# Recurrence with fewer load buffers, the scaling one step further ahead, one group of products moved, and half as many warm products of twice the length

## The chip, the cores and the metric

The program runs on one core of one Trainium2 chip. The metric is the device time of one execution in microseconds, as the median of several runs. Times inside an execution are taken from one profiled execution and counted from the start of its span.

## The reference

Three stages follow each other. The first is a linear-attention recurrence over 768 positions, for 4 sequences, 8 heads and a head size of 48:

```python
for t in range(S):
    cur = np.einsum('bhd,bhe->bhde', u[None] * kt, vt)
    y[:, :, t] = np.einsum('bhd,bhde->bhe', rt, state + cur)
    state = w[None, :, :, None] * state + np.einsum('bhd,bhe->bhde', kt, vt)
```

Its output, 3072 tokens of 384 numbers, goes through a mixture of 8 experts (hidden size 1024). Each token with a positive skip score goes to the expert with the highest logit, and `gate * (relu(x @ w1[e]) @ w2[e])` is added to it. The third stage is a soft mixture of 8 experts with 4 slots each: softmaxes of `x @ phi` over tokens and over slots, two products per slot, and a combination over slots. Everything is float32.

## The kernel before

All engines' programs are written out by hand: inside `manual_schedule` each engine executes its instructions in the order in which the Python code issues them. The part that matters here is the loop `for i in range(NT)` with 24 steps. Step `i` handles one block of 128 positions (`c`) of one sequence (`b`), all 8 heads together. For one block the work is:

- `load(j)` (L509 to L519) issues two transfers on SyncE's queue: `rk`, the block of r and k, into one of `NRK = 5` buffers `rkb`, and `kv` into one of 5 buffers with the tag `kvt`. A transfer into a buffer is issued when the last reader of its former contents is done, and SyncE's queue is in order, so it holds up all transfers behind it. In step `i` the loads of block `i + 3` are issued; the last reader of a `kvt` buffer is the second half of `av` for its block (TensorE, L753), one step after the block's own.
- `prep(j)` (L630) scales r and k by decay powers into the tile `rks` (VectorE, L635 and L636) and multiplies r with k into `pd` (GpSimd, L638). `prepk(j)` makes `kt` from `kv` (GpSimd, L644). Both are called in step `j - 1`.
- `scores(j)` (L646): 16 products `sc` (L656), which the chip's records show as 32 pairs of a weight load and a product, then for the block before `inter` (L734) and the first half of `av` (L753), then the argument `between`, then the products `ud` (L666) and their copy `dts` (ScalarE, L668).
- `trx` (transposes, L764), `upd` (products into `ud`, L679), `bonus` (a transpose, L682), `moved` (copy by ScalarE, L695), the second half of `av`.
- `past(j)` (VectorE, L705) takes the masked scores out of `sc` into `at`, and `amask(j)` (VectorE, L714) puts the diagonal in. `sc` has one buffer in PSUM, so the products `sc` of step `i + 1` wait for `past(i)`; `av` of step `i + 1` waits for `amask(i)`.

Every fourth step has routing work besides: `route1` (8 records of products `lgt`, L837, copied by ScalarE to `lgs`, L838), `route2` (transposes of `lgs`), and in the three steps after it many short VectorE instructions (`route2b`, `gates`, `places`, `route4`, `hots`). `route1(4)` is the `between` of step 21 and `route1(5)` that of step 23.

Ahead of the loop `warm(n, w)` (L498) issues `n` products of a constant with `4 * w` columns that nobody reads: `warm(44, 48)` first, and `warm(5, 48)` in step 0. From step 20 on, `wload` issues the expert weights on SyncE's queue behind the last loads of the recurrence, and `stored` writes finished tokens (`x_d`) on the same queue. Behind the loop the router finishes, tokens are gathered for the experts, and from 139.5 us on TensorE runs the experts' products.

Of the kernel before, what the change touches and what calls it, by code (L numbers as in the profile page):

```python
# [8 lines left out]
F32 = mybir.dt.float32  # L9
# [10 lines left out]
P = 128  # L20
NC_ = S // P
NT = B * NC_
DM = H * D
# [7 lines left out]
PR = 112  # L31
HT = P // 2
NWR = 7
NWARM = 44
NVX = 10
WLO, WHI = 0.8, 1.1
HF = F // 2
# [437 lines left out]
def tile_main(ctx, tc, rk, kv, wu, wcat, phi, w1, w2, v1, v2, r_in, k_in, v_in, w_in, u_in, wcn, out, dbg=None, force=False):  # L475
    nc = tc.nc
# [13 lines left out]
    PE_, DVE_, ACT_, POOL_, SP_ = (mybir.EngineType.PE, mybir.EngineType.DVE, mybir.EngineType.Activation, mybir.EngineType.Pool, mybir.EngineType.SP)  # L490
    mst = ExitStack()
    mst.enter_context(tc.manual_schedule(engines={PE_, DVE_, ACT_, POOL_, SP_}))
    NRK = 5
    ones = fp.tile([P, P], BF16, name="ones")
    nc.vector.memset(ones, float(E))

    def warm(n, w=P):

        wp = ps.tile([P, 2, 4 * P], F32, tag="y", name="wp")[:, 0, 0 : 4 * w]
        for _ in range(n):  # L500
            nc.tensor.matmul(wp, ones, ones[:, 0:w].rearrange("p (o n) -> p o n", o=1).to_broadcast([P, 4, w]), start=True, stop=True)  # L501

    warm(NWARM, 48)
    rkb = [kp.tile([PR, 2, 4, P], F32, name=f"rkb{i}") for i in range(NRK)]
    wt = kp.tile([PR, 2, 4], F32, name="wt")
    nc.sync.dma_start(out=wt, in_=wu)
# [1 line left out]
    T = {}  # L508

    def load(j, first=True, last=True):  # L510
        c, b = divmod(j, B)
        if first:
            t = T[j] = {"rk": rkb[j % NRK]}
            nc.sync.dma_start(out=t["rk"], in_=rk[c, b])
        if not last:
            return
        t = T[j]
        t["kv"] = wk.tile([P, 2, DM], F32, tag="kvt", bufs=5, name=f"kvt{j}")
        nc.sync.dma_start(out=t["kv"], in_=kv[c, b])  # L519

    load(0, last=False)
# [105 lines left out]

    yts = {}

    def prep(j):  # L630
        t = T[j]
        rkt = t["rk"]
        rks = wk.tile([PR, 2, 4, P], F32, tag="rks", bufs=3, name=f"rks{j}")
        t["rs"], t["ks"] = rks[:, 0], rks[:, 1]
        nc.vector.tensor_mul(rks[:, 0], rkt[:, 0], prt)  # L635
        nc.vector.tensor_mul(rks[:, 1], rkt[:, 1], pkt)  # L636
        t["pd"] = wk.tile([PR, 4, P], F32, tag="pd", name=f"pd{j}")
        nc.gpsimd.tensor_mul(t["pd"], rkt[:, 0], rkt[:, 1])  # L638

    def prepk(j):  # L640
        t = T[j]
        if j < NT - B:
            t["kt"] = wk.tile([P, DM], F32, tag="kt", name=f"kt{j}")
            nc.gpsimd.tensor_mul(t["kt"], t["kv"][:, 0], pktok.rearrange("t h d -> t (h d)"))  # L644
# [183 lines left out]
    def route1(g, pool=ps, tag="r"):  # L828
        c, (j0, nb) = g, GR[g]
        r = RT[c] = {}  # L830
        lgt = pool.tile([P, nb * P], F32, tag=tag, name=f"lgt{c}")
        r["lgs"] = ry.tile([P, nb * P], F32, tag="lgs", bufs=2, name=f"lgs{c}")
        yt, b0 = yts[j0 // B], j0 % B
        for q in range(2):
            for s2 in range(2):
                p = 2 * s2 + q
                nc.tensor.matmul(lgt[64 * s2 : 64 * s2 + 64, :], wcs[:, p, :], yt[:, p, b0 : b0 + nb, :].rearrange("d b t -> d (b t)"), start=(q == 0), stop=(q == 1))  # L837
        nc.scalar.copy(r["lgs"], lgt)  # L838
# [183 lines left out]
    pa = Banks(u=[(ps, "t", 1)])  # L1022
    if True:
        for i in range(NT):
            if i + 3 < NT:
                load(i + 3)
            rc, rb = divmod(i - 5, B)
            rok = 0 <= rc < NC_ - 1
            if i == 0:
                decays()  # L1030
                warm(5, 48)
                prep(0)
                prepk(0)
                for hf in range(2):
                    r0 = 64 * hf
                    nc.vector.tensor_copy(usel[r0 : r0 + D, :, hf : hf + 1], wt[r0 : r0 + D, 1, :].rearrange("p (a o) -> p a o", o=1))
            scores(i, lambda: route1(i // 2 - 6) if i in (21, 23) else None)
            if i > 1:
                trx(i - 2)
            if rok and rb == 3 or i == 22:  # L1040
                route3(rc, place=T[i]["rp"])
            if rok and rb == 2 and rc < 4:
                route2(rc)
            if i == 21:
                route2(4)
            if i == 23:
                route2(5)
            if rok and rb == 1 and rc < 4:
                route1(rc)
            if i == 0:  # L1050
                prep(1)
                prepk(1)
                for ts in spf:
                    for t in ts:
                        nc.gpsimd.memset(t[:, 4 * D :], 0.0)
            elif i + 1 < NT:
                prep(i + 1)
                prepk(i + 1)
            if i > 0:
                state(i - 1)  # L1060
            upd(i)
            if i == 22:
                c4pt = ps.tile([P, P], F32, tag="r", name="c4pt")
                nc.tensor.transpose(c4pt, c4t.rearrange("p q s -> p (q s)"), ident)
            bonus(i)
            moved(i)
            if i > 0:
                av(i - 1, 1)
            if i in (13, 17, 21, 22):
                gathered(len(LI))  # L1070
            past(i)
            if i == 22:
                nc.vector.tensor_reduce(mcs[:, 0:1], c4pt, axis=AX.X, op=ALU.max)
                dgt = rt.tile([32, 32], F32, tag="dg", bufs=1, name="dgt")
                nc.vector.tensor_scalar(dgt, ident[0:32, 0:32], mcs[0:32, 0:1], None, op0=ALU.mult)
                amask(22)
                weave("pgpgg", g=gates(4), p=places(4))
                tokens(4, nc.gpsimd)
                hots(4, range(4), nc.gpsimd)
            decayed(i)  # L1080
            if i == 21:
                nc.vector.tensor_reduce(cmax, cmg.rearrange("t g s -> t s g"), axis=AX.X, op=ALU.max)
                c4t = fourfold(nc, "t", rt, cmax)
                amask(21)
                route2b(4)
            elif rb == 0 and 1 <= rc < 4:
                route4(rc - 1)
            if i % B and 9 <= i < 22:
                hots(i // B - 2, (i % B,) if i < 20 else (2, 3), nc.vector if i < 20 else nc.gpsimd)
            if i not in (21, 22):  # L1090
                amask(i)
            if rok and rb == 2 and rc < 4:
                route2b(rc)
            if rok and rb == 3:
                weave("gpgpg", g=gates(rc), p=places(rc))
                count(rc)
                tokens(rc, nc.gpsimd)
                hots(rc, (0,) if rc < 3 else (0, 1), nc.vector if rc < 3 else nc.gpsimd)
                if rc == 3:
                    route4(3)  # L1100
            if i == 8:
                wok = rt.tile([PR, 2, 4], F32, tag="wok", bufs=1, name="wok")
                nc.vector.tensor_scalar(wok[:, 0], wt[:, 0, :], WLO, None, op0=ALU.is_ge)
                nc.vector.tensor_scalar(wok[:, 1], wt[:, 0, :], WHI, None, op0=ALU.is_le)
                wmn = mk.tile([PR, 1], BF16, name="wmn")
                nc.vector.tensor_reduce(wmn, wok, axis=AX.XY, op=ALU.min)
            if 20 <= i < 23:
                wload(i - 20)
            if i % B == 1 and 9 <= i < 25:
                stored(i - 9, B)  # L1110
            if i == 22:
                stored(16, B)
            if 3 <= i < 7:
                constants(i)
            if i == 4:
                odd = rt.tile([P, NT], F32, tag="odd", bufs=1, name="odd")
                nc.vector.tensor_reduce(odd[:, 0:1], ident.rearrange("p (a r) -> p r a", r=2)[:, 1:2], axis=AX.X, op=ALU.add)
                nc.vector.tensor_scalar(odd[:, 1:2], odd[:, 0:1], float(-NT), None, op0=ALU.mult)
                tf = rt.tile([P, 2, NT], F32, tag="tf", bufs=1, name="tf")
                nc.scalar.copy(tf, tj_i)  # L1120
                nc.vector.tensor_scalar(tj[:, 0], tf[:, 0], float(NT), odd[:, 1:2], op0=ALU.mult, op1=ALU.add)
                nc.vector.tensor_sub(tj[:, 1], tf[:, 1], tj[:, 0])
                nc.gpsimd.iota(ipl.bitcast(I32), pattern=[[E, CAP]], base=-NOROW, channel_multiplier=0)
                nc.gpsimd.tensor_copy(ipl, ipl.bitcast(I32))
                for t in tok:
                    nc.gpsimd.memset(t, 0.0)
            if i == 6:
                sf = rt.tile([P, E], F32, tag="sf", bufs=1, name="sf")
                nc.vector.tensor_reduce(sf, ident.rearrange("p (q r s) -> p s q r", q=4, s=E)[:, :, :, 0:2], axis=AX.XY, op=ALU.add)
                nc.scalar.copy(selb, sf)  # L1130
# [543 lines left out]
```

## Time and profile before

| | us |
|---|---|
| median of 3 runs | 350.14 |
| lowest and highest | 348.92, 354.14 |
| the profiled execution | 348.07 |
| its span, first to last instruction | 346.3 |

The profile gives for each engine when its instructions ran and what ended the idle time before them. `PE` is TensorE's products, `PEld` its weight loads, `DVE` VectorE, `ACT` ScalarE, `POOL` GpSimd, `SP` SyncE; a `q` behind a name is an engine's queue. A wait put down to "issue" is one for which the profile shows no releaser. The granted clock is 1.00 at 2.4 GHz and 0.50 at 1.2 GHz. The execution's own time is 1.77 us longer than its span.

### The profile page before, as it was taken

The numbers are of one execution on the slowest core, as the hardware profiler recorded it, in microseconds if no ns is written. First come the engines' busy times: TensorE is split into PE (matmuls) and PEld (weight loads), VectorE is DVE, ScalarE is ACT, GpSimd is POOL, SyncE is SP. The second block draws the span as 40 slices with busy tenths as digits, with TensorE's granted clock in tenths as the row PEclk, the third lists the DMA queues.
The fourth block names the chain that finished last, engine by engine and source line by source line (L and its number), as shares of the span: only waits on it lengthen the run. The fifth ranks groups of instructions, "written<-read, shape, count | busy, mean of one in ns | idle before, by whom it ended". The sixth has DMA issues, their size and how long they took to land.

```text
span 346.3 us, 10440 instructions
## 1 busy us (share of the span) xinstructions
PE 321.4 (93%) x4326; PEld 263.9 (76%) x4326; DVE 226.1 (65%) x510; ACT 159.5 (46%) x353; POOL 139.8 (40%) x181
## 2 busy tenths in 40 slices
PE   8699998999998999999999999999999999999950
PEld 8477776767775782999999999998999998534540
DVE  6637676896969865776675848575676845226850
ACT  3235454444543463554645546464645543121360
POOL 3939685776844544804324232525224002200000
PEclk9969999999999998999999999999999999899995
DMA  7976667684879944899788787878866749779096
GB/s 233 287 220 190 187 189 255 199 269 141 279 191 310 387 163 158 266 310 315 252 288 303 239 281 255 263 257 296 294 197 215 254 124 377 256 268 324 10 338 210
DMA packets 45735, 85.29 MB, mean 246 GB/s; under 512 B 3838, under 2 KB 26672, under 8 KB 45680
## 3 DMA queue, kind: packets, MB, share of 16 engines
q1 hardware_dynamic: 43024, 80.63, 70.8%
q0 software_dynamic: 2128, 3.74, 3.9%
q8 instruction: 36, 0.59, 0.7%
q10 hardware_dynamic: 528, 0.16, 0.2%
q14 instruction: 19, 0.16, 0.1%
HBM read 74.49 MB, written 10.10 MB: 244 GB/s over the span
## 4 chain that ended last, share of the span: by engine, by line
PE 79%; DVE 12%; issue 3%; ACT 2%; POOL 1%; ACTq 0%; DVEq 0%
PE yp L1291 7%; PE yp L1292 6%; PE yp L1293 6%; PE hp L1266 6%; PE hp L1269 6%; PE hp L1267 6%; PE yp L753 4%; PE ehp L216 4%; PE sc L656 3%; PE lgt L837 3%; PE ud L679 3%; PE trp L764 3%; PE yp L734 2%; PE wp L501 2%; PE ud L666 2%
## 5 line engine op out<-in xcount | busy, mean ns | idle before, releaser
L1266 PE MATMUL hp<-xhl,wa 128*128 128x240 f32 x192 | 46.1, 282 | 0.2 <-issue 0.2
L1291 PE MATMUL yp<-wb,hh 128*128 128x384 f32 x128 | 45.2, 353 | 0.0
L1004 DVE TENSOR_TENSOR wa<-w,wa 128x768 fp32r<-128x768 f32 x32 | 30.5, 955 | 22.4 <-ACT wa L1016 22.3
L1267 PE MATMUL hp<-xhl,wa 128*128 128x240 f32 x192 | 44.6, 275 | 0.0
L1292 PE MATMUL yp<-wb,hh 128*128 128x384 f32 x128 | 43.0, 336 | 0.0
L1293 PE MATMUL yp<-wb,hl 128*128 128x384 f32 x128 | 42.9, 335 | 0.0
L1197 POOL DMA_INDIRECT xg<-x_d,idg x16 | 19.9, 1242 | 51.9 <-DVE x L1299 38.1
L638 POOL TENSOR_TENSOR pd<-rkb 112x512 f32<-112x512 f32 x24 | 31.1, 1295 | 18.6 <-PE ud L666 15.3
L1321 POOL DMA_INDIRECT lt_d<-lsr,ids x16 | 17.7, 1106 | 50.2 <-ACT xhl L1256 28.3
L1266 PEld LDWEIGHTS hp<-xhl,wa 128*128 128x128 f32 x192 | 36.2, 189 | 0.5 <-ACT dsbv L135 0.5
L1267 PEld LDWEIGHTS hp<-xhl,wa 128*128 128x128 f32 x192 | 36.2, 189 | 0.0
L714 DVE COPY_PREDICATED at<-ih,ud 128x512 f32<-128x512 int32 x24 | 17.7, 738 | 26.0 <-ACT us L695 16.5
L1004 DVE TENSOR_TENSOR wb<-w,wb 128x768 fp32r<-128x768 f32 x32 | 30.5, 953 | 2.1 <-ACT wb L1016 1.7
L1016 ACT CAST wb<-w 128x768 fp32r<-128x768 f32 x32 | 26.8, 838 | 9.5 <-PE yp L1293 5.5
L753 PE MATMUL yp<-at,kvt 64*48 64x64 f32 (+3 forms) x800 | 27.7, 250 | 1.0 <-DVE at L714 0.4
L1276 ACT ACTIVATE hh<-hp 128x480 fp32r<-128x480 f32 x32 | 18.3, 572 | 22.2 <-PE hp L1269 20.0
L1277 DVE SCALAR_TENSOR_TENSOR hl<-hp,hh 128x480 fp32r<-128x480 f32 x32 | 20.9, 654 | 9.7 <-ACT hh L1276 9.2
L1016 ACT CAST wa<-w 128x768 fp32r<-128x768 f32 x32 | 26.9, 840 | 0.0
L1291 PEld LDWEIGHTS yp<-wb,hh 128*128 128x128 f32 x128 | 24.0, 188 | 3.6 <-issue 3.5
L1269 PE MATMUL hp<-xhl,wa 128*128 128x240 f32 x192 | 26.7, 275 | 0.0
L656 PE MATMUL sc<-rks 48*64 48x128 f32 (+1 forms) x768 | 22.1, 252 | 4.5 <-DVE at L705 2.3
L753 PEld LDWEIGHTS yp<-at,kvt 64*48 64x48 f32 (+1 forms) x800 | 22.2, 125 | 5.3 <-issue 1.6
(346 smaller groups left out, 697.1 us busy)
## 6 DMA issues: line engine op xcount, KB each, us to landing
w<-in_w_dram SPq DMA_DIRECT2D x32, 768.0 KB
v<-in_v_dram SPq DMA_DIRECT2D x29, 768.0 KB
rkb<-in_rk_dram SPq DMA_DIRECT2D x24, 448.0 KB
kvt<-in_kv_dram SPq DMA_DIRECT2D x24, 384.0 KB
x_d<-x SPq DMA_DIRECT2D x5, 768.0 KB
out_dram<-ob SPq DMA_DIRECT2D x5, 768.0 KB
x<-in_v_dram SPq DMA_DIRECT2D x2, 768.0 KB
x_d<-x SPq DMA_DIRECT2D x2, 384.0 KB
```

Source lines behind the costliest of these rows:

```text
L638: nc.gpsimd.tensor_mul(t["pd"], rkt[:, 0], rkt[:, 1])
L656: nc.tensor.matmul(sc[c0 : c0 + HT, g, blocks(p, z), :], ks[r0 : r0 + D, p, HT * z : HT * z + HT], rs[r0 : r0 + D, p, HT * z :], start=Tru ...
L753: nc.tensor.matmul(d, kvt[s0 : s0 + HT, 1, h * D : h * D + m], w, start=(c == ph == z == 0), stop=(ph == z == 1))
L1004: nc.vector.tensor_sub(lv, sl, hv.bitcast(F32))
L1016: nc.scalar.copy(hv, sl)
L1266: nc.tensor.matmul(hp[:, f, 0:ROOM], hi[:, k, fs], xh[:, k, 0:ROOM], start=(k == 0 and f == 0), stop=False)
L1267: nc.tensor.matmul(hp[:, f, 0:ROOM], lo[:, k, fs], xh[:, k, 0:ROOM], start=False, stop=False)
L1269: nc.tensor.matmul(hp[:, f, 0:ROOM], hi[:, k, fs], xl[:, k, 0:ROOM], start=False, stop=(k == 2 and f == 1))
L1277: nc.vector.scalar_tensor_tensor(l, p, 0.0, h.bitcast(F32), op0=ALU.max, op1=ALU.subtract)
L1291: nc.tensor.matmul(YP[e][bl], hh[:, f, bs], hi[:, f, :], start=st, stop=False)
L1292: nc.tensor.matmul(YP[e][bl], hh[:, f, bs], lo[:, f, :], start=False, stop=False)
L1293: nc.tensor.matmul(YP[e][bl], hlo[:, f, bs], hi[:, f, :], start=False, stop=en)
```

## The change

The `rkb` buffers go from 5 to 3 and the `kvt` buffers from 5 to 4. The scaling leaves `prep` for a function `scaled`, with 4 buffers for `rks` in place of 3. `scaled(i + 2)` is called in step `i`: behind `past(i)` from step 3 on, behind `amask(i)` in steps 0 to 2 (there `scaled(0)` and `scaled(1)` stand where `prep` had them). `load(3)` moves behind the first `prep` and `prepk`, since it now reuses the first `rkb` buffer. `route1(4)` moves from the middle of `scores(21)` to behind it. `warm(44, 48)` becomes `warm(22, 96)` and `warm(5, 48)` becomes `warm(2)` with 512 columns.

```diff
-NWARM = 44
+NWARM = 22
...
-    NRK = 5
+    NRK = 3
...
-    warm(NWARM, 48)
+    warm(NWARM, 96)
...
-        t["kv"] = wk.tile([P, 2, DM], F32, tag="kvt", bufs=5, name=f"kvt{j}")
+        t["kv"] = wk.tile([P, 2, DM], F32, tag="kvt", bufs=4, name=f"kvt{j}")
...
+    def scaled(j):
+        if j >= NT:
+            return
+        t = T[j]
+        rkt = t["rk"]
+        rks = wk.tile([PR, 2, 4, P], F32, tag="rks", bufs=4, name=f"rks{j}")
+        t["rs"], t["ks"] = rks[:, 0], rks[:, 1]
+        nc.vector.tensor_mul(rks[:, 0], rkt[:, 0], prt)
+        nc.vector.tensor_mul(rks[:, 1], rkt[:, 1], pkt)
+
     def prep(j):
         t = T[j]
         rkt = t["rk"]
-        rks = wk.tile([PR, 2, 4, P], F32, tag="rks", bufs=3, name=f"rks{j}")
-        t["rs"], t["ks"] = rks[:, 0], rks[:, 1]
-        nc.vector.tensor_mul(rks[:, 0], rkt[:, 0], prt)
-        nc.vector.tensor_mul(rks[:, 1], rkt[:, 1], pkt)
...
-            if i + 3 < NT:
+            if 0 < i < NT - 3:
                 load(i + 3)
...
-                warm(5, 48)
+                warm(2)
+                scaled(0)
                 prep(0)
                 prepk(0)
+                load(3)
...
-            scores(i, lambda: route1(i // 2 - 6) if i in (21, 23) else None)
+            scores(i, lambda: route1(5) if i == 23 else None)
+            if i == 21:
+                route1(4)
...
+                scaled(1)
                 prep(1)
...
             past(i)
+            if i > 2:
+                scaled(i + 2)
...
+            if i <= 2:
+                scaled(i + 2)
```

VectorE's order in steps 7 and 8, before; the number behind a tile's name is its block, and L635 and L636 are the scaling:

```order
L635 TENSOR_TENSOR rks8_880<-rkb3_132,prt_212 112x512
L636 TENSOR_TENSOR rks8_880<-rkb3_132,prt_212 112x512
L705 TENSOR_TENSOR at7_841<-sc7_824,mh_192 128x2x256
L714 COPY_PREDICATED at7_841<-ih_193,ud7_860 128x2x256
...
L901 SCALAR_TENSOR_TENSOR oh0_923<-lgp0_873,m20_921 128x32
L635 TENSOR_TENSOR rks9_983<-rkb4_133,prt_212 112x512
L636 TENSOR_TENSOR rks9_983<-rkb4_133,prt_212 112x512
L705 TENSOR_TENSOR at8_945<-sc8_928,mh_192 128x2x256
L714 COPY_PREDICATED at8_945<-ih_193,ud8_964 128x2x256
```

The same place after the change, where the scaling is L637 and L638, `past` L711 and `amask` L720:

```order
L711 TENSOR_TENSOR at7_817<-sc7_800,mh_168 128x2x256
L637 TENSOR_TENSOR rks9_882<-rkb0_107,prt_188 112x512
L638 TENSOR_TENSOR rks9_882<-rkb0_107,prt_188 112x512
L720 COPY_PREDICATED at7_817<-ih_169,ud7_836 128x2x256
...
L907 SCALAR_TENSOR_TENSOR oh0_899<-lgp0_849,m20_897 128x32
L711 TENSOR_TENSOR at8_921<-sc8_904,mh_168 128x2x256
L637 TENSOR_TENSOR rks10_985<-rkb1_108,prt_188 112x512
L638 TENSOR_TENSOR rks10_985<-rkb1_108,prt_188 112x512
L720 COPY_PREDICATED at8_921<-ih_169,ud8_940 128x2x256
```

The two scaling instructions of a step stand behind `past` in place of ahead of it, and are for the block after the next; `amask` stands behind both as before.

TensorE's order in the middle of step 21, before; `lgt4` are the products of `route1(4)`, `ud21` those whose copy `dts21` is transposed in the last row:

```order
L753 MATMUL yp20_2222<-at20_2128,kvt20_1817 48x64 x4
L837 MATMUL lgt4_2239<-yt4_1895,wcs_140 64x512 x4
L666 MATMUL ud21_2246<-pd21_2169,usel_142 32x128 x4
L764 MATMUL trp19_2253<-ident_149,yt4_1895 128x112 x4
L865 MATMUL lgp4_2259<-ident_149,lgs4_2240 128x128 x4
L682 MATMUL ud21_2246<-ident_149,dts21_2251 128x128
```

The same place after the change:

```order
L759 MATMUL yp20_2198<-at20_2104,kvt20_1793 48x64 x4
L672 MATMUL ud21_2215<-pd21_2142,usel_118 32x128 x4
L843 MATMUL lgt4_2222<-yt4_1868,wcs_116 64x512 x4
L770 MATMUL trp19_2229<-ident_125,yt4_1868 128x112 x4
L871 MATMUL lgp4_2235<-ident_125,lgs4_2223 128x128 x4
L688 MATMUL ud21_2215<-ident_125,dts21_2220 128x128
```

`ud21` and `lgt4` change places; what stands between `lgt4` and the transposes `lgp4` that need its copy is now `trp19` alone.

## Rows read from the trace of the kernel before

**Rows 1.** Time windows of the whole program: busy us by engine (instructions), TensorE clock, DMA share, GB/s
```profile
28.00:124.00 96.00, 90.69 (x2229) 68.42 (x2229) 74.86 (x194) 45.72 (x121) 63.89 (x85) 1.00 0.76 241
...
139.50:300.00 160.50, 160.38 (x1204) 152.30 (x1208) 105.60 (x195) 84.96 (x166) 50.78 (x54) 1.00 0.81 271
```

**Rows 2.** Timeline of the start: start, length, engine, line; wait in brackets
```profile
9.49 1.28 POOL L638 TENSOR_TENSOR pd<-rkb 112x512 f32<-112x512 f32 x1
...
9.84 0.64 PE L679 MATMUL ud<-kvt,kt 128*64 128x48 f32 x16 [0.43 <-POOL kt L644]
...
14.57 0.51 PE L656 MATMUL sc<-rks 48*64 48x128 f32 x12
...
17.30 1.01 PE L656 MATMUL sc<-rks 48*64 48x64 f32 x19 [2.22 <-issue]
...
24.38 0.54 PE L753 MATMUL yp<-at,kvt 64*64 64x128 f32 x10 [0.32 <-issue]
...
29.77 0.42 PEld L679 LDWEIGHTS ud<-kvt,kt 128*64 128x64 f32 x12 [0.25 <-issue]
```

**Rows 3.** The page's list of DMA queues: packets, MB, share of 16 engines
```profile
q8 instruction: 36, 0.59, 0.7%
```

**Rows 4.** The page's list of transfers: KB of one
```profile
rkb<-in_rk_dram SPq DMA_DIRECT2D x24, 448.0 KB
kvt<-in_kv_dram SPq DMA_DIRECT2D x24, 384.0 KB
```

**Rows 5.** Timeline of SyncE's queue at the start
```profile
8.29 0.33 SPq L514 DMA_DIRECT2D rkb<-in_rk_dram  x1
...
15.29 0.77 SPq L514 DMA_DIRECT2D rkb<-in_rk_dram  x1
...
23.38 0.37 SPq L514 DMA_DIRECT2D rkb<-in_rk_dram  x1
```

**Rows 6.** Time windows from the start, and around the half clock
```profile
0.00:10.70 10.70, 9.14 (x114) 8.25 (x114) 7.26 (x24) 3.27 (x10) 5.50 (x17) 1.00 0.83 237
0.00:17.30 17.30, 12.97 (x221) 11.12 (x222) 11.66 (x31) 5.13 (x15) 11.37 (x30) 0.98 0.91 260
0.00:24.40 24.40, 19.75 (x350) 16.56 (x350) 14.35 (x36) 7.53 (x21) 13.64 (x32) 0.86 0.87 240
17.30:23.40 6.10, 6.10 (x109) 5.01 (x112) 1.70 (x3) 1.92 (x5) 2.27 (x2) 0.50 0.79 208
23.40:27.00 3.60, 3.28 (x92) 2.45 (x87) 1.59 (x3) 1.52 (x5) 1.55 (x2) 1.00 0.76 232
```

**Rows 7.** TensorE's waits from 28 to 124 us: total us, times, longest
```profile
PE sc L656 <- DVE at L705: 2.3, 5, 0.9
PE yp L734 <- issue: 0.7, 1, 0.7
PE ud L679 <- issue: 0.7, 1, 0.7
PE yp L753 <- DVE at L714: 0.4, 1, 0.4
```

**Rows 8.** A window inside the recurrence, of steps 7 to 9
```profile
45.00:55.20 10.20, 9.14 (x264) 7.30 (x256) 9.71 (x32) 5.12 (x13) 8.58 (x13) 1.00 0.78 239
```

**Rows 9.** Instructions that write or read the scaled tile: ns min/median/max
```profile
L635 DVE TENSOR_TENSOR rks<-rkb,prt x24: 667/677/687, 6.7 to 116.6; 112x512 f32<-112x512 f32 x24
```

**Rows 10.** Timeline of steps 21 to 23
```profile
108.02 0.90 PE L656 MATMUL sc<-rks 48*64 48x128 f32 x32 [0.88 <-DVE at L705]
...
110.01 1.94 PE L837 MATMUL lgt<-yt,wcs 112*64 112x512 f32 x8 [0.32 <-DVE ltt L957]
...
118.51 0.90 PE L656 MATMUL sc<-rks 48*64 48x128 f32 x32 [0.58 <-DVE at L705]
```

**Rows 11.** Timeline of the warm products
```profile
1.13 6.29 PE L501 MATMUL wp<-ones 128*128 128x192 bf16 x44 [1.13 <-DVE ones L495]
```

**Rows 12.** A window after the last loads of the recurrence
```profile
125.00:129.00 4.00, 3.74 (x84) 3.52 (x76) 3.12 (x15) 2.46 (x8) 1.30 (x2) 1.00 0.02 7
```

## The prediction

> **What bounds the kernel now.** I read the time windows first. From 139.5 us to 300 TensorE is busy for 160.38 of 160.50 us [rows 1]; nothing of the change stands there, so that part keeps its length and what is won earlier passes through. From 28 to 124 us, inside the recurrence, TensorE is busy for 90.69 of 96 us [rows 1], so about 5 us are open there at most. The start is the other place. In the timeline the reader sees TensorE stop after 12 of the 32 products of `sc` of step 2 and go on at 17.30 us after 2.22 us of "issue", which means that no engine and no data is named as the cause [rows 2]. Then its clock: 0.50 from 17.3 to 23.4 us, 1.00 behind it [rows 6]. A product with its weight load takes 6.10 / 109 = 0.056 us in the slow stretch and 3.60 / 92 = 0.039 us behind it.
>
> What is it waiting for? The next "issue" waits of this kind stand at 24.38 and 29.77 us [rows 2]. By the product counts of the windows, 350 - 221 = 129 products start between the resumption at 17.30 and shortly after that at 24.38 [rows 6], so a block is 128 products, or 256 instructions with their weight loads. The queue named "instruction" moves 0.59 MB in 36 packets, 16 KB each [rows 3]; if one packet is one block, an instruction has 64 bytes. I read the stops as program code that comes late, behind the data transfers.
>
> The transfers fit that. I take it that a block is asked for when the one before it begins, 128 products earlier. For the stop that ends at 17.30 this is about 9.84 us [rows 2]. By then SyncE has issued 6 `rk` and 5 `kv` [rows 5], which are 4608 KB or 4.72 MB [rows 4], and 237 GB/s x 9.84 us = 2.33 MB have moved [rows 6]: 2.4 MB stand ahead, and the block takes 7.5 us. For the next, asked for at 17.30, 7 and 6 are issued, 5.57 MB, 4.50 MB are moved, 1.07 MB stand ahead and it takes 7.1 us until 24.38. For the third, at 24.38, 8 and 7, 6.42 MB, 5.86 moved, 0.56 ahead, and 5.4 us until 29.77. With less ahead it comes sooner.
>
> The Trainium skill says otherwise in "Runtime: NRT & Kernel Launch", section "Instruction fetch mechanics": instructions come in 16 KiB blocks of 256, the next is fetched while the present one runs, and the crossing is mostly hidden. The block size agrees with the counts here; that it is hidden does not agree with 2.22 us at 17.30. By its rule the term of the start below would be zero.
>
> **The change part by part.**
>
> *Warm products.* 44 x 192 columns become 22 x 384 and 5 x 192 become 2 x 512: 8448 columns as before, and 1024 for 960. The first group takes 6.29 us [rows 11], and I leave its length as it is. What goes is 25 products, so each block border falls 25 products later in the work.
>
> *Fewer load buffers.* The fourth `rk` now reuses the first buffer; the sixth did so before and was issued at 8.29 us [rows 5], so the fourth `rk` and `kv` are issued at 8.3 to 9 us. The fifth `rk` waits for the second `pd`, which ends at 9.49 + 1.28 = 10.77 us [rows 2]. The block in question is asked for 25 products later than before, 9.84 + 25 x 0.039 = 10.8 us. By then 4 and 4 are issued, 3.41 MB, and 237 x 10.7 = 2.54 MB are moved [rows 4, 6]: 0.87 MB ahead, or 1.33 if the fifth `rk` gets in first. Between the two measured blocks (0.56 MB 5.4 us, 1.07 MB 7.1 us) that is 6.4 us, so it arrives at about 17.2; with 1.33 MB at 17.9. TensorE gets to this border 25 products after 15.08 us (17.30 - 2.22), at 16.1: a stop of 1.1 us, between 0 and 1.8, in place of 2.22. Before, the same place in the work was reached at 17.30 + 25 x 0.056 = 18.7. The gain is 18.7 - 17.2 = 1.5 us.
>
> *Clock.* The slow stretch followed TensorE's stop. Of it 23.4 - 18.7 = 4.7 us are left behind that place, 84 products, and at full clock they would take 84 x 0.017 = 1.4 us less. A stop of 1.1 us may or may not cost the clock; I take half, 0.7 us, with ends 0 and 1.4. The stops of 0.32 and 0.25 us [rows 2] become shorter with less ahead of them: 0.3. Start together: 1.5 + 0.7 + 0.3 = 2.5 us, from 0.5 (late block, clock lost) to 4.6 (no stop at all).
>
> *Scaling a step ahead.* The two instructions take 0.68 us each [rows 9] and run as often as before. They go from ahead of `past` to behind it, so `past` ends up to 1.3 us earlier and `sc` of the next step need not wait. That wait is 2.3 us over five steps [rows 7]. Two of them are 0.88 us in step 21 and 0.58 in step 23 [rows 10]. In step 21 the products `lgt` wait for VectorE anyway (0.32 us on L957), and VectorE has no less to do ahead of L957, so 0.3 comes out. In step 23 no scaling is left to do and all 0.6 comes out. The other three, 0.8 us, lie in stretches such as 45.0 to 55.2, where VectorE is busy for 9.71 of 10.20 us [rows 8]. There it has the same instructions to run up to the last `amask`, for which `av` waits, and TensorE waited 0.4 us for one already [rows 7]. The wait moves from `past` to `amask`, and I count 0. If VectorE had slack, all 0.8 would come out; if the scaling holds `amask` back, the same is lost.
>
> *Step 21.* `lgt` of `route1(4)` behind `ud`: the same products, and TensorE can run `ud` while `lgt` waits. This is the 0.3 counted above, not another. The copy of `lgt` now has only `trx` to hide behind ahead of the transposes; the price is between 0 and 0.4 us, and I take 0.
>
> *Block borders later on.* From 28 to 124 us there are 2229 / 128 = 17 borders. Two of them cost 0.7 us each [rows 7]. All of them move by 25 products, and so against the transfers that each step issues. Some of 1.4 us goes, and other borders get late. Above all the expert weights, issued behind the last `kv`, go out a step later: the `kv` buffers are 4, not 5. So the borders of the last three steps meet them. Price from -1.4 to +2.0; I take 0. The weights themselves have room: the transfers are idle at 0.02 from 125 to 129 us [rows 12], nearly the step of 96 / 20 = 4.8 us by which they are later.
>
> **Sum.** 2.5 + 0.9 = 3.4 us off the profiled execution's 348.07 us (span 346.3, 1.77 around it): 344.7. The three runs shown are 348.92, 350.14 and 354.14; the profiled execution is 0.9 below the lowest and 2.1 below the median. I add 1.5 of this and forecast 346.2 us, 1.1% below the median of 350.14. About 2% is what a measurement of this kernel can tell from no change: under 343.1 us is faster, over 357.1 slower.
>
> **The rivals.**
>
> *The stop goes altogether and the clock holds.* For it: the queue is emptier by 4.72 - 3.41 = 1.3 MB less what moves in 1 us. Against it: 0.87 MB ahead is near the 1.07 MB of a block that took 7.1 us. Then the start gives 4.6, and with 0.9 and half of the 1.4 us of later borders 6.2: 341.9 in the profiled execution, 343 as a median.
>
> *Nothing comes out.* The block waits behind the fifth `rk`, the clock is lost again, `amask` takes over the waits of `past`, and new borders cost what old ones did. 0.5 + 0.9 - 1.4 = 0: 349.5 us.
>
> *The stop at 17.30 is not late code.* Then 25 fewer products and an emptier queue change nothing at the start, and 0.9 is left: 347.2 in the profiled execution, 348.7 as a median. Against it: the spacing of exactly one packet's worth of instructions. This is what the page's rule in the Trainium skill comes to.
>
> *Loads too late: slower.* The `rk` of block j + 5 is issued behind the `kv` that waits for `av` at the end of step j + 1, and the scaling needs it in the middle of step j + 3, where before there were more than two steps more. That is 1.5 steps, 7 us at 4.8 us a step. A step's two transfers are 832 KB, 3.5 us at 241 GB/s [rows 4, 1]; a store of `x_d` ahead of them (as large) makes it 7 us, with the landing still to come. The scaling then holds up `amask` on VectorE. If that costs 1 us in each of the four steps with a store and in the four short steps 3 to 6, it is 8 us, less 3.4: 353 us. It decides from the point where a load takes over 1.5 steps to land. Against it: no wait for a load stands among TensorE's waits [rows 7], and behind the scaling there is a whole step until `sc` needs it.
>
> **How the numbers follow.** Forecast 0.49, stop gone 0.19, nothing 0.15, not late code 0.07, loads late 0.10. The likeliest case's own range is 344 to 348.5. The range that holds 8 of 10 leaves out the lower half of the second case and most of the last: 342.8 to 350.2 us. Under 343.1 lies a little over half of the second case and a rest of the first: 0.13. Over 357.1 lies a third of the last case: 0.03. Within 2%: 0.84.
>
> **What would show it.** Right: the long "issue" wait stands some 5 products into `av` behind a finished `sc` of step 2, is 0.5 to 1.8 us, and ends near 17 us; no wait of `sc` for L711, but one of `av` for L720 in steps 10, 14 or 18; the gap ahead of `sc` of step 23 is gone; experts from about 136 us. Wrong: a stop at the same product as before, a stop of over 2 us, a clock of 0.50 for as long as before, a wait of VectorE or GpSimd for `rkb` or `kvt`, or experts that start after 139 us.

## The result and the profile after

| | before | after |
|---|---|---|
| median (us) | 349.37 (20 runs, 345.61 to 354.14) | 343.49 (20 runs, 340.03 to 348.5) |
| ratio, with 95% interval | | 0.986, 0.983 to 0.9889 |
| profiled execution, span (us) | 348.07, 346.3 | 341.5, 339.5 |
| mean granted clock of the profiled execution | 0.967 | 0.982 |

The change makes the kernel 1.4% faster by the ratio and 1.7% by the medians. The forecast was 346.2 us in a range of 342.8 to 350.2: the result is inside, 2.7 us below the forecast and 0.7 us above the range's low end. A ratio leaves out the runs that are over 1.5% above the fastest of their kernel, so it hangs on that one run (of before it kept 22 of 29 runs in one group of the experiments below and 11 or 12 of 29 in the two others), and the medians, over all runs, are given beside it.

TensorE's waits from 28 to 124 us, after (total us, times, longest), beside [rows 7]:

```profile
PE yp L759 <- DVE at L720: 2.1, 3, 1.1
PE trp L770 <- issue: 0.7, 1, 0.7
PE yp L759 <- issue: 0.5, 1, 0.5
```

The reader sees that no wait of `sc` for `past` (2.3 us before) is left, and that waits of `av` for `amask` (L720) stand in its place, 2.1 us for 0.4. "issue" has 1.2 us for 1.7 (1.4 in [rows 7], and one more wait of 0.3 at the transposes of L764).

The timeline of the start, after, beside [rows 2]:

```profile
14.53 0.88 PE L662 MATMUL sc<-rks 48*64 48x128 f32 x32
...
16.58 0.55 PE L759 MATMUL yp<-at,kvt 64*48 64x128 f32 x11 [0.68 <-issue]
...
19.18 0.88 PE L662 MATMUL sc<-rks 48*64 48x128 f32 x32
...
26.40 0.88 PE L662 MATMUL sc<-rks 48*64 48x128 f32 x32
...
112.54 0.90 PE L662 MATMUL sc<-rks 48*64 48x128 f32 x32
...
118.35 0.32 PE L759 MATMUL yp<-at,kvt 64*48 64x64 f32 x5 [0.55 <-issue]
...
123.97 1.49 PE L129 MATMUL dpst<-x,ltt 128*32 128x385 f32 x12
...
133.11 0.38 PE L1281 MATMUL hp<-xhl,wa 128*128 128x240 f32 x1 [0.24 <-ACT xhl L1271]
```

And the rows of the timeline before that answer to the first and the last steps:

```profile
18.11 0.95 PE L753 MATMUL yp<-at,kvt 64*64 64x128 f32 x14
...
22.62 1.22 PE L656 MATMUL sc<-rks 48*64 48x128 f32 x32
...
30.90 0.88 PE L656 MATMUL sc<-rks 48*64 48x128 f32 x32
...
129.07 2.72 PE L129 MATMUL dpst<-x,ltt 128*32 128x385 f32 x12
```

`sc` of step 2 now runs through, and the stop of 2.22 us is one of 0.68 behind it, inside `av`. `sc` of step 3 starts 22.62 - 19.18 = 3.44 us earlier, that of step 5 30.90 - 26.40 = 4.50, that of step 23 118.51 [rows 10] - 112.54 = 5.97. In the step after it, where a stop of 0.55 us is new, 0.87 is given back (129.07 - 123.97 = 5.10), and then `dpst` takes 1.49 us for 2.72. The windows give the clock:

```profile
17.30:23.40 6.10, 6.02 (x181) 4.90 (x177) 4.14 (x7) 3.42 (x9) 4.76 (x5) 1.00 0.76 206
...
123.00:130.00 7.00, 6.30 (x78) 2.76 (x75) 4.38 (x21) 4.32 (x9) 2.67 (x4) 1.00 0.60 210
```

```profile
129.20:132.60 3.40, 3.40 (x24) 0.90 (x24) 1.51 (x8) 2.75 (x4) 0.02 (x1) 0.50 0.41 125
```

The first fence is after, the second before. From 17.3 to 23.4 us TensorE starts 181 products for 109 [rows 6], at 1.00 for 0.50; and `dpst` ran at 0.50 before and at 1.00 now.

Of the loads, SyncE's queue after shows

```profile
10.94 0.33 SPq L514 DMA_DIRECT2D rkb<-in_rk_dram  x1
...
14.78 0.33 SPq L519 DMA_DIRECT2D kvt<-in_kv_dram  x1
15.21 0.37 SPq L514 DMA_DIRECT2D rkb<-in_rk_dram  x1
```

The fifth `rk` goes out at 10.94 us and the sixth at 15.21, where the sixth went at 8.29 and the seventh at 15.29 [rows 5].

### The profile page after: what moved, and what is told of

Read it like the earlier page. It is cut to its first block, busy times and chain, and to the rows that moved or that the text cites. A ratio compares the mean times of both kernels' runs of the same rounds, so it can differ in the third digit from the quotient of the medians.

```text
span 339.5 us, 10394 instructions
## 1 busy us (share of the span) xinstructions
PE 317.7 (94%) x4301; PEld 258.2 (76%) x4301; DVE 226.2 (67%) x510; ACT 159.8 (47%) x353; POOL 139.8 (41%) x181
## 4 chain that ended last, share of the span: by engine, by line
PE 75%; DVE 14%; issue 3%; ACT 2%; DMA 2%; SPq 0%; POOL 0%; ACTq 0%; DVEq 0%; POOLq 0%
PE yp L1306 7%; PE yp L1307 7%; PE yp L1308 7%; PE hp L1281 6%; PE hp L1284 6%; PE hp L1282 6%; PE yp L759 4%; PE ehp L216 4%; PE lgt L843 3%; PE sc L662 3%; PE ud L685 2%; PE trp L770 2%; DVE at L720 2%; DMA kvt<-in_kv_dram 2%; PE xtp L1269 2%
## 5 line engine op out<-in xcount | busy, mean ns | idle before, releaser
L759 PE MATMUL yp<-at,kvt 64*48 64x64 f32 (+3 forms) x800 | 26.9, 246 | 3.7 <-DVE at L720 2.1
L720 DVE COPY_PREDICATED at<-ih,ud 128x512 f32<-128x512 int32 x24 | 17.6, 735 | 17.7 <-ACT us L701 11.4
L759 PEld LDWEIGHTS yp<-at,kvt 64*48 64x48 f32 (+1 forms) x800 | 21.2, 121 | 8.8 <-DVE at L720 3.3
L650 POOL TENSOR_TENSOR kt<-kvt,pktok 128x384 f32<-128x384 f32 x20 | 20.1, 1006 | 12.0 <-DMA kvt<-in_kv_dram 7.4
```

The costliest lines, as they stand in the source:

```text
L720: nc.vector.copy_predicated(t["at"][:, :, 0:4], ih_i.rearrange("s (a o t) -> s a o t", a=1, o=1).to_broadcast([P, 2, 4, HT]), t["dtk"].rea ...
L759: nc.tensor.matmul(d, kvt[s0 : s0 + HT, 1, h * D : h * D + m], w, start=(c == ph == z == 0), stop=(ph == z == 1))
```

## The experiments

| kernel | median us (runs) | ratio to before, 95% | ratio of the medians |
|---|---|---|---|
| the change (from the result above) | 343.49 (20) | 0.986, 0.983 to 0.9889 | 0.983 |
| before + warm alone | 347.98 (12) | 0.9971, 0.9924 to 1.0018 | 0.995 |
| before + fewer load buffers alone | 345.51 (6) | 0.9898, 0.984 to 0.9955 | 0.988 |
| before + early loads held | 348.24 (12) | 0.9946, 0.9906 to 0.9987 | 0.996 |
| before + scaling ahead alone (4 `rk`) | 346.59 (12) | 0.9936, 0.9892 to 0.998 | 0.991 |
| before + 4 `rk` buffers (control) | 349.43 (12) | 1.0078, 1.0029 to 1.0126 | 0.999 |
| before, blocks 2 to 11 not loaded | 342.42 (4) | 0.9874, 0.9696 to 1.0052 | 0.979 |
| after, warm undone | 344.28 (12) | 0.9894, 0.9841 to 0.9946 | 0.985 |
| after, buffers undone (4 `rk`, 5 `kv`) | 347.39 (12) | 0.9993, 0.9912 to 1.0074 | 0.993 |
| after, scaling undone | 343.91 (12) | 0.9915, 0.9857 to 0.9973 | 0.983 |
| after, `route1(4)` undone | 344.68 (12) | 0.9899, 0.985 to 0.9948 | 0.986 |
| after, 5 `kv` buffers | 348.37 (12) | 1.0017, 0.9964 to 1.007 | 0.996 |

One more run told nothing and stands at the end. Kernels measured together share 29 runs of before (medians 349.68 to 349.81). The changed kernel was not measured again in these groups, so a difference against it is one of medians from different groups.

### What the stops at the start are

A border is the place where TensorE's program enters its next block of 128 products.

**No loads.** Blocks 2 to 11 are not loaded and use the data of blocks 0 and 1; later loads as before.

```diff
+    keep = {}
...
     def load(j, first=True, last=True):
+        if 2 <= j < 12:
+            T[j] = {"rk": rkb[j % 2], "kv": keep[j % 2]}
+            return
...
+        keep.setdefault(j, t["kv"])
```

> The kernel before, but blocks 2 to 11 are not loaded: they use the data of blocks 0 and 1 again, so that part of the computation has other input, with the same instructions on TensorE, VectorE, ScalarE and GpSimd; 20 transfers less, nearly nothing moves between 8 and 45 us. Theory A (code is late because of the load transfers): no issue wait of over 0.1 us for TensorE from 10 to 50 us, clock 1.00 there, sc of step 12 some 5.5 to 7 us earlier than before (2.2 for the stop, 2.4 for the half clock, 1 to 2 for the later stops). Theory F (a block of code takes a fixed time from asking, whatever the transfers do): the stop of 1.5 to 2.2 us at the twelfth product of sc of step 2 stays, sc of step 12 earlier by 0 to 3 us.

The windows and the timeline of this kernel:

```profile
10.70:28.00 17.30, 16.50 (x477) 12.92 (x469) 12.86 (x25) 8.56 (x23) 15.09 (x27) 1.00 0.04 12
28.00:36.00 8.00, 7.96 (x191) 5.79 (x194) 4.82 (x12) 4.04 (x10) 5.75 (x8) 1.00 0.83 246
42.80:49.60 6.80, 6.80 (x122) 5.80 (x116) 3.83 (x16) 2.03 (x5) 3.52 (x5) 0.50 0.01 2
```

```profile
14.34 0.88 PE L661 MATMUL sc<-rks 48*64 48x128 f32 x32
...
17.97 0.88 PE L661 MATMUL sc<-rks 48*64 48x128 f32 x32
...
39.26 0.40 PE L661 MATMUL sc<-rks 48*64 48x128 f32 x6
41.31 0.76 PE L661 MATMUL sc<-rks 48*64 48x128 f32 x24 [1.65 <-issue]
```

With 12 GB/s from 10.7 to 28 us the stop is gone, the clock stays 1.00, and `sc` of step 3 starts at 17.97, 4.65 us earlier than before. Then a burst of a store and four loads (246 GB/s from 28 to 36 us) is followed by a new stop of 1.65 us in the middle of `sc` of step 8, where the kernel before has none, and that by half clock. So the stops come with the transfers; a fixed time from asking (theory F) is out. About half of the gain was lost again to this second stop: `sc` of step 8 starts 5.60 us earlier than before (39.26 for 44.86), that of step 12 only 2.79 (61.82 for 64.61), where theory A had 5.5 to 7.

That what comes late is code, the traces show directly, for they hold the time of each packet of the queue "instruction". In before, packets end at 15.69, 22.87 and 28.27 us, and TensorE goes on at 17.30, 24.38 and 29.77; after the change one ends at 15.05, and TensorE goes on at 16.58; here, at 39.90 and 41.31. In the profiles of before, of after and of the eleven other kernels of the table, TensorE's products have 38 stops of over 0.2 us from 14 to 125 us that are put down to "issue", and each ends 1.25 to 1.65 us behind the end of such a packet. Not every "issue" is one: a wait of 0.43 us at 13.31 us after, and two of 0.85 and 0.24 us ahead of 136.96 and 139.51 us in before, are at no packet.

**Warm alone.**

```diff
-NWARM = 44
+NWARM = 22
...
-    warm(NWARM, 48)
+    warm(NWARM, 96)
...
-                warm(5, 48)
+                warm(2)
```

> The kernel before with the longer warm products alone (22 of 384 columns, 2 of 512), so that every block border of TensorE's code falls 25 products later. Theory A (code blocks late behind the load transfers): the queue at the start is as full as before (2.54 MB moved of 4.72 at 10.8 us, 2.2 MB ahead, against 2.4), so the long stop stays, now 5 products into av behind a finished sc of step 2 and between 1.5 and 2.2 us long; the half clock behind it stays too; total -1.0 to +0.5 us against before. Theory B (the warm products themselves keep the clock up: the gain is theirs alone): stop as long or not, but no half clock from 17 to 23 us, total -3 us or more. Theory C (the scaling ahead is the gain): 0.

```profile
17.98 0.55 PE L753 MATMUL yp<-at,kvt 64*48 64x128 f32 x11 [1.63 <-issue]
```

The stop stands 25 products later, in `av`, and is 1.63 us long, as theory A has it. The half clock behind it was expected and did not come in this execution. The ratio is 0.9971 with an interval that holds 1 (0.995 by the medians): by itself the border's place is worth 0.3 to 0.5% or nothing.

**Fewer load buffers alone.**

```diff
-    NRK = 5
+    NRK = 3
...
-        t["kv"] = wk.tile([P, 2, DM], F32, tag="kvt", bufs=5, name=f"kvt{j}")
+        t["kv"] = wk.tile([P, 2, DM], F32, tag="kvt", bufs=4, name=f"kvt{j}")
...
-            if i + 3 < NT:
+            if 0 < i < NT - 3:
                 load(i + 3)
...
                 prepk(0)
+                load(3)
```

> The kernel before with fewer load buffers alone (3 rk, 4 kv, load(3) behind the first prep). Theory A: the border stays after 12 products of sc of step 2, its block is asked for with 1.1 MB ahead in place of 2.4 and comes at 16 to 17 us in place of 17.3; TensorE is there at 15.1, so the stop is 0.9 to 1.9 us in place of 2.22, the half clock may stay; total -0.5 to -3 us. Theory B (warm products hold the clock): stop and half clock as before, total 0. Theory D (loads too late): +1 us or more, from waits of VectorE and GpSimd for rkb and kvt.

```profile
14.52 0.51 PE L656 MATMUL sc<-rks 48*64 48x128 f32 x12
16.49 0.61 PE L656 MATMUL sc<-rks 48*64 48x64 f32 x19 [1.46 <-issue]
```

The stop is at the twelfth product as before and ends at 16.49 us for 17.30, 1.46 us long; theory A's numbers. The clock held. 1.0% (0.45 to 1.6) comes from this edit alone, the largest of the single parts, from six runs; the interval overlaps that of the scaling alone.

**Early loads held, later ones not.** Blocks 3 and 4 use the first two `rk` buffers, then all five are used; five `kv` buffers.

```diff
-            t = T[j] = {"rk": rkb[j % NRK]}
+            t = T[j] = {"rk": rkb[(0, 1, 2, 0, 1, 3, 4)[j] if j < 7 else (2, 0, 1, 3, 4)[(j - 7) % NRK]]}
...
-            if i + 3 < NT:
+            if 0 < i < NT - 3:
...
+                load(3)
```

> The kernel before with 5 rk and 5 kv buffers as before, but blocks 3 and 4 put into the first two rk buffers and load(3) behind the first prep, so that the early loads alone are held back and the later ones have all buffers. Theory A with the start alone: the same as with fewer buffers, -0.5 to -3 us, stop at 15.1 us shorter than 2.22. If the fewer buffers act later in the loop (transfers spread differently against the block borders), this one gives nothing or another amount, 1 us or more apart from it.

```profile
10.66 0.67 PE L679 MATMUL ud<-kvt,kt 128*64 128x48 f32 x16 [1.41 <-POOL kt L644]
...
11.66 1.56 PE L656 MATMUL sc<-rks 48*64 48x128 f32 x32
```

0.5% (1.6 us by the medians), inside what was expected, but not by the step that the theory named: in the profiled execution TensorE waited 1.41 us for `kt` early, ran at half clock from 11.2 to 21.5 us, and came so late to the border that the code was there. By the medians it gives 2.7 us less than fewer buffers throughout, which the expectation had as the sign that they act later in the loop; but the early wait makes another start of it, and the intervals overlap, so this run doesn't tell the start from the rest. It shows that a wait for data can be followed by half clock as a wait for code can.

### What the parts are worth in the changed kernel

**Buffers undone**: 4 `rk` and 5 `kv`, `load(3)` early.

```diff
-    NRK = 3
+    NRK = 4
...
-        t["kv"] = wk.tile([P, 2, DM], F32, tag="kvt", bufs=4, name=f"kvt{j}")
+        t["kv"] = wk.tile([P, 2, DM], F32, tag="kvt", bufs=5, name=f"kvt{j}")
...
-            if 0 < i < NT - 3:
+            if i + 3 < NT:
...
-                load(3)
```

> The changed kernel with 4 rk and 5 kv buffers and load(3) where it was before. If the fewer buffers are most of the gain: 346.5 to 348 us, +3 us or more against the changed kernel, mean clock 0.966 or so, with a stop of 1.5 us or more in av of step 2. If the parts add (1.0% for the buffers alone): 346 to 347.5. If nothing hangs on them: 343 to 344.5.

```profile
17.68 0.55 PE L759 MATMUL yp<-at,kvt 64*48 64x128 f32 x11 [1.81 <-issue]
...
27.30 1.52 PE L662 MATMUL sc<-rks 48*64 48x128 f32 x32
```

The stop of 1.81 us in `av` is back, `sc` of step 4 starts at 27.30 us (22.82 in the changed kernel) at half speed, and by the ratio nothing of the 1.4% is left (0.9993, with an interval down to 0.9912), by the medians 0.7 of 1.7%. So more than half of the gain hangs on the buffers; how much the other three parts are worth without them this run does not settle.

**Five `kv` buffers** in the changed kernel, and nothing else:

```diff
-        t["kv"] = wk.tile([P, 2, DM], F32, tag="kvt", bufs=4, name=f"kvt{j}")
+        t["kv"] = wk.tile([P, 2, DM], F32, tag="kvt", bufs=5, name=f"kvt{j}")
```

> The changed kernel with 5 kv buffers for 4 (3 rk as it has), a version that may beat both: the waits of GpSimd for kv (7.4 us in the changed kernel's profile) should go, the expert weights go out a step earlier. If these waits cost something: -0.5 to -1 us, 342.5 to 343. If what counts is that few transfers stand ahead of TensorE's code: 0 to +1.5 us, with longer issue waits in the loop.

TensorE and SyncE's queue of this kernel:

```profile
16.85 0.55 PE L759 MATMUL yp<-at,kvt 64*48 64x128 f32 x11 [0.99 <-issue]
...
19.46 0.88 PE L662 MATMUL sc<-rks 48*64 48x128 f32 x32
...
21.83 0.29 PE L685 MATMUL ud<-kvt,kt 128*64 128x48 f32 x2
25.52 0.56 PE L685 MATMUL ud<-kvt,kt 128*48 128x48 f32 x14 [3.40 <-issue]
```

```profile
11.01 0.43 SPq L519 DMA_DIRECT2D kvt<-in_kv_dram  x1
13.20 0.33 SPq L514 DMA_DIRECT2D rkb<-in_rk_dram  x1
14.73 0.33 SPq L519 DMA_DIRECT2D kvt<-in_kv_dram  x1
16.52 0.33 SPq L514 DMA_DIRECT2D rkb<-in_rk_dram  x1
19.71 0.33 SPq L519 DMA_DIRECT2D kvt<-in_kv_dram  x1
21.50 0.33 SPq L514 DMA_DIRECT2D rkb<-in_rk_dram  x1
```

```profile
16.80:23.90 7.10, 5.19 (x126) 3.96 (x127) 4.02 (x7) 2.77 (x7) 3.68 (x4) 1.00 1.04 256
26.20:29.50 3.30, 3.30 (x81) 2.87 (x80) 1.50 (x3) 1.28 (x3) 2.49 (x6) 0.50 0.42 123
```

This run decides most. Up to step 3 it is as the changed kernel (19.46 and 19.18 us). But the fifth `kv` goes out at 11.01 us, not at 14.78, and all behind it earlier; the transfers move 256 GB/s without a gap from 16.8 to 23.9 us (the changed kernel: 209), and TensorE stops for 3.40 us. The packet of code ends at 23.95 us, and TensorE goes on 1.57 us behind it, at 25.52, soon at half clock. One buffer of 384 KB costs all of the gain by the ratio (1.0017, 0.9964 to 1.007) and three quarters of it by the medians (0.996 for 0.983). The expectation had the direction, 0 to +1.5 us; it is +4.9 by the medians. GpSimd's waits for `kvt` fall from 7.4 to 2.1 us, and that gains nothing.

**Scaling alone**, with 4 `rk` buffers, and its **control**, 4 `rk` buffers without the scaling. The edit is `scaled` as in the change, with

```diff
-    NRK = 5
+    NRK = 4
...
```

> The kernel before with the scaling one step ahead alone (4 rks buffers, and 4 rk buffers for 5, since the memory holds no more). Prediction: sc waits for past no longer, -0.9 us; the wait moves to amask. Theory C (the scaling is the gain): -4 us or more. Theory E (VectorE-bound: nothing): 0 within 0.5. The stop at the start stays over 1.5 us by all of them, as the rk buffer missing holds back one transfer of 448 KB at most.

> The kernel before with 4 rk buffers and nothing else: the control for the run with the scaling alone (346.6 us, 0.994), which had them too. If the scaling is worth the 0.9 us of the prediction, this one takes about 347.5 to 348; if the scaling gave all of it, 349.5; if it gave nothing, 346.6.

TensorE's waits from 28 to 124 us with the scaling ahead:

```profile
PE yp L759 <- DVE at L720: 1.2, 3, 0.6
PE yp L759 <- issue: 0.8, 1, 0.8
PE lgt L843 <- DVE ltt L963: 0.6, 1, 0.6
```

The two were measured in different groups, and their ratios (0.9936 and 1.0078) are further apart than their medians, which are 2.8 us apart: between the 0.9 of the prediction and the 4 or more of theory C, and theory E is out. The control takes the 349.5 us of "the scaling gave all of it". Of the 2.3 us of waits of `sc` for `past` none is left, the waits for `amask` rise from 0.4 to 1.2 only, and that of `lgt` from 0.3 to 0.6: 1.2 us net in the loop. The rest of the difference stands at the start, with the scaling (first fence) and in the control:

```profile
16.95 0.84 PE L662 MATMUL sc<-rks 48*64 48x64 f32 x19 [1.57 <-issue]
```

```profile
17.75 1.01 PE L656 MATMUL sc<-rks 48*64 48x64 f32 x19 [2.31 <-issue]
```

The packet of code ends at 15.40 us with the scaling ahead and at 16.17 in the control. Why it comes sooner, and whether it does in every execution, I leave open.

**Scaling undone** in the changed kernel (back in `prep`, 3 `rks`):

> The changed kernel with the scaling back in prep, ahead of past, and 3 rks buffers. Prediction's term: +0.9 us, 344.4, sc waits for past again (2.3 us). If it is worth what the scaling alone gave beside one rk buffer less (0.6%): +2 us, 345.5. If the wait only moved to amask: 0.

```profile
PE sc L656 <- DVE at L705: 2.2, 6, 0.6
PE yp L734 <- issue: 1.5, 1, 1.5
PE yp L753 <- DVE at L714: 0.9, 2, 0.5
```

0.9915 for 0.986, and +0.4 us by the medians: between the 0 and the 0.9 expected, with intervals that overlap. The waits for VectorE are 3.1 us for 2.1.

**Warm undone** and **`route1(4)` undone**, each the reverse of its hunk in the diff:

> The changed kernel with the short warm products of before (44 of 192 columns, 5 of 192): borders back at their old products. If the parts add (warm alone gave 0.3%, with an interval about 0): +0.5 to +1.5 us against the changed kernel, a stop of some 1.5 us after 12 products of sc of step 2. If warm and buffers are only worth it together, as the prediction's start term has it: +2 us or more and a half clock from 17 us.

> The changed kernel with route1(4) back in the middle of scores(21). Prediction: it only goes with the scaling in step 21, 0 to +0.3 us, 343.5 to 343.9. Rival: the copy of lgt has less to hide behind in the changed order, so that this one is 0.2 to 0.4 us faster.

TensorE with the short warm products:

```profile
16.69 0.61 PE L662 MATMUL sc<-rks 48*64 48x64 f32 x19 [1.73 <-issue]
```

The stop is back behind the twelfth product of `sc` of step 2, 1.73 us long, and half clock follows from 18.4 to 21.9 us. 0.9894 and 0.9899: +0.8 and +1.2 us by the medians, with intervals that reach past 0.986. For `warm` the time is where the parts adding up has it, and not the 2 us of "only worth it together", though that case's half clock came in this execution. For `route1(4)` neither sign can be read; the profiled execution of it has 0.6 us of wait of `lgt` for VectorE where the changed kernel has 0.2.

**A run that told nothing.** The attempt at the early loads alone, with the buffers of `kv` named by hand:

```diff
+    kvb = [kp.tile([P, 2, DM], F32, name=f"kvt{i}") for i in range(5)]
...
-            t = T[j] = {"rk": rkb[j % NRK]}
+            t = T[j] = {"rk": rkb[j % 3 if j < 9 else (3, 4, 0, 1, 2)[(j - 9) % NRK]]}
...
-        t["kv"] = wk.tile([P, 2, DM], F32, tag="kvt", bufs=5, name=f"kvt{j}")
+        t["kv"] = kvb[j % 4 if j < 8 else (4, 0, 1, 2, 3)[(j - 8) % 5]]
...
```

> The kernel before with its five rk and five kv buffers, of which blocks 0 to 8 use three and blocks 0 to 7 four: the early loads go out as with the fewer buffers, the later ones run as far ahead as before. If the fewer buffers act at the start alone: 345 to 346 us, as with fewer buffers throughout (345.5), sc of step 5 some 3.4 us earlier than before. If they act later (borders in steps 8 to 22, and the half clock at 129 us): step 5 earlier by 3.4 us all the same, and 1 us or more of it given back behind step 8; 346.5 to 348.

```profile
PE yp L754 <- DMA kvt<-in_kv_dram: 9.1, 3, 7.8
```

It took 361.38 us. Written so, the load of block j + 4 stands in the program ahead of the second half of `av` of block j, so for blocks 0 to 3 that half waits for the new data and uses it: the 9.1 us of waits in the first 60 us. It says nothing on the question. Whether the buffers matter only at the start, or in steps 8 to 22 too, is left open.

## Why the prediction was right, and where its sizes were off

**The reading of "issue" as late code** holds: the kernel without loads has no such stop from 10.7 to 28 us, the burst that follows makes one, and each stop ends 1.25 to 1.65 us behind a packet of code. The rule in the Trainium skill ("Runtime: NRT & Kernel Launch", section "Instruction fetch mechanics"), that the crossing is mostly hidden, agrees with the stretch of 12 GB/s and with most of the recurrence (3 stops at 17 borders from 28 to 124 us, at 241 GB/s), and not with the stops of 2.22, 1.65 and 3.40 us. The data ahead of a block did not give its time: 2.4 MB at 237 GB/s would be 10 us and 0.56 MB 2.4, for the 7.5 and 5.4 in the prediction. When a block is asked for, no record shows.

**Warm products and fewer buffers, 1.5 us.** The stop stands where it was forecast, 5 products into `av`. Forecast were 1.1 us and an end at 17.2; measured are 0.68 and 16.58. The fifth `rk` got in at 10.94 us, just behind the supposed asking time of 10.8, and the block came 0.6 us sooner than between the two blocks of before that I used. In before the same product starts at 18.24 us, the fourth of the 14 at 18.11, and not at 18.7: the mean of 0.056 us, taken over the whole slow stretch, is too long for these 25 products. So the place is reached 18.24 - 16.58 = 1.66 us earlier. That 1.5 comes close is luck: both ends were put about half a microsecond too late.

**Clock, 0.7 us.** This is the term that was mis-sized. I took half of 1.4; the profiled execution keeps the clock, and that gives 2.2 us, more than the upper end: 3.44 - 1.66 = 1.78 up to `sc` of step 3, and 0.4 from there to the end of the half clock at 23.4. From 18.24 us on TensorE runs 92 products at half clock, and what they lose is 2.2 / 92 = 0.024 us each, for the 84 and 0.017 in the prediction.

**Later stops at the start, 0.3 us.** From step 3 to 5 another 4.50 - 3.44 = 1.06 us come out. The stops at 24.38 and 29.77 us [rows 2] are gone, 0.32 and, by the length of `ud` (0.97 us for 0.64), 0.33; the other 0.4 is the clock's. The start term is thus 1.66 + 2.2 + 0.65 = 4.5 us for 2.5, at the end of its bounds (0.5 to 4.6).

**Scaling, 0.9 us.** The prediction's mechanism is what the rows show: no wait of `sc` for L711, waits of `av` for L720 in its place (at 51.35, 89.73 and 103.55 us, in steps 10, 18 and 21), the gap ahead of `sc` of step 23 gone. In the profiled execution it comes to 2.3 + 0.4 - 2.1 = 0.6 us net. In step 21 `lgt` waits 0.2 us for 0.3, and the transposes `lgp` wait 0.2 us for its copy, which I had at 0. Undoing the scaling costs 0.4 us by the medians; alone it gave more than 0.9, 1.2 us in the loop. That the other 0.8 us would be lost to `amask` is so in the changed kernel and not so in the one with the scaling alone.

**Later borders, 0.** Within the loop it is nearly right: 1.2 us of "issue" for 1.7. Behind step 23 a late block gives back 0.55 of the 0.87 us; then the half clock of 129.2 us is not there, 1.2 us, which no term had. That this comes of the change is not shown: a half clock that starts between 123 and 130 us stands in five of the thirteen profiles (before, warm alone, scaling alone, no loads, buffers undone), and not in the control with 4 `rk`. From 4.50 at step 5 on: +1.47 to step 23, -0.87, +1.23 for `dpst`, 6.3 in all; the experts start at 133.11 us, where the forecast had about 136.

**Sum.** The profiled execution is 348.07 - 341.5 = 6.6 us shorter, for 3.4 forecast: 2.0 of the difference are the start and 1.2 the half clock at 129.2 us. The median lies 2.0 us above the profiled execution, for the 1.5 that I added.

**The rivals.** "The stop goes altogether and the clock holds" named the time (343) and half of its condition: the clock held, the stop did not go. "The stop is not late code" is out by the kernel without loads and by the packets. "Loads too late" is there as waits, without a price that the trace shows. (Its sum is uneven: 8 - 3.4 on 348.07 is 352.7 in the profiled execution, and 354.2 with the 1.5 that the other cases add.) The waits of GpSimd and VectorE after:

```profile
POOL kt L650 <- DMA kvt<-in_kv_dram: 7.4, 8, 2.2
POOL pd L644 <- DMA rkb<-in_rk_dram: 5.3, 4, 3.4
```

```profile
DVE rks L637 <- DMA rkb<-in_rk_dram: 1.3, 2, 1.1
```

Such waits stood in the prediction as a sign that it is wrong, and they came; it was a poor sign, since GpSimd waits 3.0 us for the first `rkb` in before too. TensorE's list has no wait for a load, and behind VectorE's two waits, which end at 33.96 and 96.32 us, no wait of TensorE follows in the same step. With a fifth `kv` buffer the first row is 2.1 us, and the kernel is slower. What I argued as a price, less read ahead, is where most of the gain comes from.

**Clock and chance.** One execution is not the kernel: runs of the changed one lie between 340.03 and 348.5 us. Over 20 runs its mean granted clock is 0.973, over 29 runs of before 0.964, with fewer buffers alone 0.975, with buffers undone or a fifth `kv` 0.968. So the gain of the clock isn't that of one profile alone.

## What to carry to other kernels

When TensorE stops with "issue" as the cause, count the products between two such stops, and see when the packets of the queue "instruction" end and what transfers are under way. Here the count was 128, each stop ended 1.25 to 1.65 us behind a packet, and the loads, issued as early as buffers allowed, made the code late. Read-ahead beyond what its reader needs gained nothing here: a fifth `kv` buffer took GpSimd's waits from 7.4 to 2.1 us, and the kernel got slower. So try fewer buffers until an engine that matters waits, and judge by the medians of many runs, since one kernel's runs spread by 8 us (340.03 to 348.5). Fewer and longer dummy products moved the borders at the same warm time; that this pays by itself was not shown (0.9971, 0.9924 to 1.0018).

## What was not expected

- One 384 KB buffer more took back most of the gain (1.0017 for 0.986, by the medians 0.996 for 0.983); in the profiled execution through a single stop of 3.40 us at 25.5 us and the half clock behind it.
- Which stops were followed by half clock is not plain from their length: those of 2.22, 2.31 and 3.40 us were; those of 0.68, 0.99, 1.46 and 1.63 us were not; those of 1.57, 1.65, 1.73 and 1.81 us were again, and so were the wait of 1.41 us for `kt` and, with the scaling undone, one of 1.48 us that ends at 96.76 us.
- The half clock at 129.2 us in before, 12 products of `dpst` in 2.72 us for 1.49, has no stop of TensorE just ahead of it: from 123 to 130 us TensorE is busy for 6.74 of 7.00 us. What decides it is open.
- Taking one `rk` buffer away (4 for 5) did not make the kernel faster, and taking two `rk` and one `kv` away made it 1.0% faster. Whether the one buffer made it slower is not shown: the ratio says 0.8% (1.0078, 1.0029 to 1.0126), and the medians of all runs are nearly the same, 349.43 and 349.72 us.
